# Scores and maxima of an attention stage put into one area of five PSUM banks, with waits kept by bank

## The chip, the cores and the metric

One core of a Trainium2 chip. The metric is the device time of one execution in microseconds (us). PE is the matmul engine (TensorE), PEld its weight load, DVE the vector engine, ACT the scalar engine, POOL GpSimd, SP the queue that issues all transfers. PSUM has eight banks of 512 fp32 columns; matmuls write there, and ACT and DVE read there.

## The reference

Block-sparse attention followed by a two-layer network. 32 heads (batch 4 by 8 heads), 768 positions, head size 64:

```python
scores = scale * np.matmul(q, k.transpose(0, 1, 3, 2))
scores = np.where(mask, scores, -1000000000.0)
scores = scores - np.max(scores, axis=-1, keepdims=True)
attn = np.exp(scores)
attn = attn / (np.sum(attn, axis=-1, keepdims=True) + 1e-09)
x = np.matmul(attn, v)            # then heads side by side: 3072 tokens x 512
h = x @ w_in                      # 512 x 2048
out = (h - np.tanh(h)) @ w_out    # 2048 x 512
```

## The kernel before, in words

The attention runs in 96 steps (`NSTEP`), three to a head; step s works for head s // 3. A step takes two tiles of 128 keys, x = 0 and 1. For each, `scores` writes 128 keys by 768 queries into PSUM as four matmuls (two of 512 columns and two of 256, each pair summing a main and a correction product, L445 and L446), `expo` (ACT, L449) takes the exponential of them into the SBUF tile `pe`, `p_high` (ACT, L455) rounds that to fp16, and `p_low` (POOL, L464) makes the rest. `accum(s)` then multiplies both with the values: 72 short matmuls into the bank `pav` (L478, L481, L482).

The row maxima that are subtracted are found ahead of that. For head h the steps 3h-6 to 3h-4 compute the same scores the other way round, query tile by query tile: `smax(h, t)` is two matmuls (L412) for each of the six tiles t, `maxima` a DVE reduction (L418), two tiles at a time. `turn_max` (PE, L426) transposes the six columns of maxima, `neg_max` (DVE, L430) negates them, and `put_max` (SP, L436) sends them as one row into the operand that `scores` of head h reads. `v_all` and `v_scale` (L382, L386) find a scale for the values of a pair of heads in a corner of the same PSUM place.

PSUM before: `bank0` and `bank1` for the network and the weights, `pst` (two banks) for the scores, of which 768 columns are used, `psm` (three banks, 1536 columns) for the maxima of two tiles, `pav` one. There is one place for scores: `scores` of the next tile waits until `expo` has read the last one.

Every operation is given to a planner (`Plan`) with a due time, an engine, an assumed duration, and names of what it reads and writes (`("pst",)`, `("psm",)`). The planner plays the engines forward, and on each picks the operation with the smallest due time among those that can start within a short time of the earliest. The result is one fixed order for each engine (`in_order`); the waits themselves come from the tile framework, which knows who touched each tile. Where the planner sees PE idle before 110 us of its own time, `KeepBusy` adds dummy matmuls into `pav` (L197).

From step 28 on, parts of the network (`FFN`) are mixed into the attention; until step 25 weights are split into two parts (`convert`, `res_hi`, `res_lo`). What is left of the network runs after the attention, on PSUM that the attention gave back.

Of the kernel before, what the change touches and what calls it, by code (L numbers as in the profile page):

```python
# [22 lines left out]
P = 128  # L23
# [26 lines left out]
BUSY = (14, 110.0, 0.85, 0.2)  # L50
WSTEP = (2, 5, 8, 11, 14, 17, 20, 23)
# [129 lines left out]

class KeepBusy:
# [71 lines left out]
def attention(ctx, tc, plan, qk, v, samp, blocks, xscr, ident, ffn):  # L254
# [4 lines left out]
    pst = ps.tile([P, 1024], F32, name="pst")  # L259
    psm = ps.tile([P, W2], F32, name="psm")  # L260
# [109 lines left out]
    TM, TV = slice(0, 128), slice(128, 256)  # L370
# [7 lines left out]
    def v_tmp(pr):  # L378
        return psm[:, TV] if pr else ffn.hb[1][:, TV]

    def v_all(pr):
        nc.tensor.matmul(v_tmp(pr), lhsT=ams[pr].to_broadcast([P, P]), rhs=ident, start=True, stop=True)  # L382

    def v_scale(pr):
        sb = sbs[pr] = p2.tile([P, 1], F32, tag="sb", name=f"sb{pr}", bufs=4)
        nc.vector.tensor_reduce(out=sb, in_=v_tmp(pr), op=ALU.max, axis=AX.X)  # L386
        sbi = sb.bitcast(I32)
# [17 lines left out]
    def smax(h, t, o=None):  # L405
        s = h % 4
        if t == 0 and h:
            mcs[h] = p2.tile([P, T], F32, tag="mc", name=f"mc{h}", bufs=3)
        b0 = t % 2 * S if o is None else 0
        o = psm if o is None else o  # L410
        for c0, c1 in ((0, 512), (512, S)) if b0 == 0 else ((0, 256), (256, S)):
            nc.tensor.matmul(  # L412
                o[:, b0 + c0 : b0 + c1], lhsT=sB[s][0:88, t * P : (t + 1) * P], rhs=sA[s][0:88, c0:c1], start=True, stop=True
            )

    def maxima(h, t, o=None):
        if o is None:
            nc.vector.tensor_reduce(  # L418
                out=mcs[h][:, t - 1 : t + 1], in_=psm.rearrange("p (x s) -> p x s", x=2), op=ALU.max, axis=AX.X
            )  # L420
        else:
            m = mcs[h][:, t : t + 1] if h else zmc[:, t, 96:97]
            nc.vector.tensor_reduce(out=m, in_=o[:, 0:S], op=ALU.max, axis=AX.X)

    def turn_max(h):
        nc.tensor.transpose(psm[0:T, TM], mcs[h], ident)  # L426

    def neg_max(h):
        nm = p2.tile([T, P], F32R, tag="nm", name=f"nm{h}")
        nc.vector.tensor_scalar(  # L430
            out=nm, in0=psm[0:T, TM], scalar1=-1.0, scalar2=8.0 * PBITS * math.log(2.0), op0=ALU.mult, op1=ALU.add
        )
        nms[h] = nm
# [6 lines left out]
    def scores(s, x):  # L440
# [3 lines left out]
        for q in (slice(0, 512), slice(512, S)):  # L444
            nc.tensor.matmul(pst[:, q], lhsT=sC[c][:, kc], rhs=sD[c][:, q], start=True, stop=False)  # L445
            nc.tensor.matmul(pst[:, q], lhsT=sA[a][0:97, kc], rhs=sB[a][0:97, q], start=False, stop=True)  # L446

    def expo(s, x):
        nc.scalar.activation(out=pe[s % 2][:, x * S : (x + 1) * S], in_=pst[:, 0:S], func=AF.Exp, scale=0.125)  # L449
# [53 lines left out]
    def at(due, f, *args):  # L503
# [32 lines left out]
        elif n == "v_all":  # L536
            eng, dur, r, w = "PE", 0.3, [("am", args[0] % 2)], [("psm",) if args[0] else ("bank", 1)]
        elif n == "v_scale":
            eng, dur, r, w = "DVE", 0.55, [("psm",) if args[0] else ("bank", 1)], [("sb", args[0] % 4)]
# [5 lines left out]
        elif n == "smax":  # L545
            h, t = args[:2]
            eng, dur = "PE", 0.345
            r, w = [(z, h % 4) for z in ("A", "B", "mA", "mB")], [(args[2],) if len(args) > 2 else ("psm",)]
        elif n == "maxima":
            h, t = args[:2]  # L550
            eng, dur = "DVE", dve(768 if len(args) > 2 else 1536) + 0.07
            r, w = [(args[2],) if len(args) > 2 else ("psm",)], [("mc", h % 3, t)]
        elif n == "turn_max":
            eng, dur, r, w = "PE", 0.1, [("mc", args[0] % 3, t) for t in range(T)], [("psm",)]
        elif n == "neg_max":
            eng, dur, r, w = "DVE", 0.25, [("psm",)], [("nm", args[0] % 2)]
        elif n == "put_max":
            dur, r, w = 0.1, [("nm", args[0] % 2)], [("row", args[0] % 4)]
        elif n == "scores":
            s, x = args  # L560
            h = s // 3
            eng, dur, w = "PE", 0.69, [("pst",)]
            r = [(z, h % 4) for z in ("A", "B", "mA", "mB", "row")] + [(z, h % 2, q) for z in "CD" for q in (0, 64)]
        elif n == "expo":
            eng, dur, r, w = "ACT", act(768), [("pst",)], [("pe", args[0] % 2, args[1])]
# [52 lines left out]
    tiles = {"psm": psm, "pst": pst}  # L618
    for t in range(T):
        o, k = ("psm", "pst")[t % 2], -70 + t  # L620
        r = [(z, 0) for z in ("A", "mA", "mB")] + [("B", 0, 0) if t < 2 else ("B", 0)]
        add(k, "PE", 0.345, smax, (0, t, tiles[o]), r, [(o,)])
        add(k + 0.0001, "DVE", dve(768) + 0.07, maxima, (0, t, tiles[o]), [(o,), ("z",)], [("mc", 0, t)])
# [4 lines left out]
    for t in range(T):  # L628
        r = [(z, 1) for z in ("A", "B", "mA", "mB")] + ([] if t else [("pst",)])
        add(0.011 + 0.0002 * t, "PE", 0.345, smax, (1, t), r, [("psm",)])  # L630
        if t % 2:
            at(0.0111 + 0.0002 * t, maxima, 1, t)
# [30 lines left out]
    for h in range(2, NHEAD):  # L663
# [17 lines left out]
    for s in range(NSTEP):  # L681
        for x in range(2):
            at(s + (0.01, 0.065)[x], scores, s, x)
# [423 lines left out]
```

## Time and profile before

| | |
|---|---|
| time, median of 3 runs | 942.32 us (940.71 to 942.59) |
| time of the profiled execution | 942.21 us |
| its span, first to last instruction | 940.4 us |
| PE, DVE, ACT, POOL busy, share of the span | 96%, 76%, 70%, 53% |
| steps 15 to 27 of the attention | 86.1 to 141.4 us of the span |

The span is 1.8 us shorter than the time of the same execution. Matmuls are pipelined, so PE's busy time counts overlaps once and is not its work: how much PE could still take is read from the spacing of its instructions. The shares are averages over stages with different limits.

### The profile page before, as it was taken

The page shows a single profiled execution, that of the slowest core. Times are in us where ns is not written, and L with a number is a line of the kernel's source. Part 1 is how long each engine was busy: PE and PEld are TensorE (multiplying, and loading weights), DVE is VectorE, ACT ScalarE, POOL GpSimd, SP SyncE. Part 2 cuts the span into 40 slices and gives each one's busy share as a digit, 9 for nine tenths or more (in the row PEclk, how much of TensorE's full clock was granted, in tenths as well). Part 3 has the DMA queues.
Part 4 walks back from the last instruction along what each step waited for, and adds up shares of the span by engine and source line. Part 5 has one row for each costly group of instructions (what it writes and reads, how often), then busy time and mean ns, then how long its engine had stood idle before and what let it go on. Part 6 is the DMA issues. An engine that isn't in the chain of part 4 may idle for free.

```text
span 940.4 us, 18434 instructions
## 1 busy us (share of the span) xinstructions
PE 905.7 (96%) x7253; PEld 750.2 (80%) x7253; DVE 711.5 (76%) x1000; ACT 656.9 (70%) x964; POOL 494.2 (53%) x324
## 2 busy tenths in 40 slices
PE   8999989998999999999999999999999999999997
PEld 4778778877888778888877877787888888888885
DVE  6999778779787778887369999976676666666765
ACT  5888888878788888888866566665555555555553
POOL 5678888777867868668843444432222222222221
PEclk9999999999999999999999999999999999999999
DMA  8878669657895666665333222221220401300201
GB/s 216 232 205 211 163 153 299 159 129 209 232 291 132 148 195 160 179 142 179 99 125 105 90 89 90 91 90 45 86 94 1 177 3 52 128 1 1 90 0 45
DMA packets 57678, 120.75 MB, mean 128 GB/s; under 512 B 6170, under 2 KB 26836, under 8 KB 56568
## 3 DMA queue, kind: packets, MB, share of 16 engines
q1 hardware_dynamic: 57592, 119.58, 44.7%
q8 instruction: 57, 0.93, 0.4%
q14 instruction: 29, 0.24, 0.1%
HBM read 55.68 MB, written 26.21 MB: 87 GB/s over the span
## 4 chain that ended last, share of the span: by engine, by line
PE 60%; DVE 24%; ACT 6%; DMA 5%; issue 3%; SPq 1%; POOL 1%; DVEq 0%; POOLq 0%; ACTq 0%
PE bank L811 16%; PE pst L445 7%; PE pst L446 6%; PE psm L412 4%; PE pf L848 4%; PE pf L846 4%; PE pf L847 4%; PE pav L478 3%; ACT pe L449 3%; PE pav L481 3%; PE pav L482 3%; DVE t L837 3%; DVE mc L418 3%; DVE bank L833 3%; DVE bank L835 3%
## 5 line engine op out<-in xcount | busy, mean ns | idle before, releaser
L464 POOL TENSOR_TENSOR pl<-pe,ph 128x768 f16<-128x768 f32 x192 | 329.9, 1732 | 111.9 <-ACT ph L455 76.1
L841 POOL TENSOR_TENSOR gl<-t,gh 128x512 fp32r<-128x512 f32 x96 | 125.8, 1310 | 303.3 <-ACT gh L839 239.0
L449 ACT ACTIVATE pe<-pst 128x768 f32<-128x768 f32 x192 | 155.3, 809 | 64.5 <-PE pst L446 61.3
L418 DVE TENSOR_REDUCE mc<-psm 128x2 f32<-128x1536 f32 x93 | 163.0, 1753 | 38.0 <-PE psm L412 37.5
L455 ACT ACTIVATE ph<-pe 128x768 f16<-128x768 f32 x192 | 159.3, 841 | 2.9
L445 PE MATMUL pst<-slab 128*128 128x512 f32 (+1 forms) x384 | 142.8, 372 | 12.3 <-ACT pe L449 10.1
L831 ACT ACTIVATE u<-u,bias 128x512 f32<-128x512 f32 x96 | 69.4, 723 | 113.1 <-DVE bank L833 113.0
L825 DVE TENSOR_TENSOR t<-t,bank 128x512 f32<-128x512 f32 x96 | 65.7, 684 | 91.3 <-ACT t L823 91.2
L446 PE MATMUL pst<-slab 97*128 97x512 f32 (+1 forms) x384 | 123.6, 343 | 0.0
L478 PE MATMUL pav<-vhl,ph 128*128 128x65 f16 x1152 | 117.6, 194 | 0.0
L481 PE MATMUL pav<-vhl,ph 128*128 128x64 f16 x1152 | 116.7, 195 | 0.2 <-DVE vhl L399 0.2
L482 PE MATMUL pav<-vhl,pl 128*128 128x65 f16 x1152 | 116.2, 193 | 0.0
L478 PEld LDWEIGHTS <-ph 128*128 128x128 f16 x1152 | 105.8, 97 | 7.0 <-issue 3.5
L839 ACT ACTIVATE gh<-t 128x512 fp32r<-128x512 f32 x96 | 60.5, 631 | 68.0 <-DVE t L837 67.9
L482 PEld LDWEIGHTS <-pl 128*128 128x128 f16 x1152 | 107.2, 99 | 0.3 <-issue 0.3
L481 PEld LDWEIGHTS <-ph 128*128 128x128 f16 x1152 | 107.2, 97 | 0.1
L445 PEld LDWEIGHTS pst<-slab 128*128 128x128 f32 x384 | 73.0, 190 | 34.1 <-ACT pe L449 21.1
L412 PE MATMUL psm<-slab 88*128 88x512 f32 (+1 forms) x378 | 87.0, 349 | 3.6 <-DVE mc L418 1.7
L846 PE MATMUL pf<-wx,gh 128*128 128x512 f32 x216 | 84.3, 390 | 2.1 <-DVE ob L907 2.0
L848 PE MATMUL pf<-wx,gl 128*128 128x512 f32 x216 | 84.1, 390 | 0.7 <-POOL gl L841 0.7
L847 PE MATMUL pf<-wx,gh 128*128 128x512 f32 x216 | 84.1, 389 | 0.0
L446 PEld LDWEIGHTS pst<-slab 97*128 97x128 f32 x384 | 73.6, 192 | 11.3
(136 smaller groups left out, 1874.1 us busy)
## 6 DMA issues: line engine op xcount, KB each, us to landing
slab<-hm SPq DMA_DIRECT2D x124, 192.0 KB
slab<-lo SPq DMA_DIRECT2D x63, 192.0 KB
raw<-qk SPq DMA_DIRECT2D x15, 768.0 KB
stage<-w_in SPq DMA_DIRECT2D x16, 512.0 KB
stage<-w_out SPq DMA_DIRECT2D x16, 512.0 KB
xsav<-xbuf SPq DMA_DIRECT2D x4, 2048.0 KB
rawv<-v SPq DMA_DIRECT2D x16, 384.0 KB
xscr<-xq SPq DMA_DIRECT2D x16, 384.0 KB
```

Of the source, the lines that this page charges most:

```text
L412: nc.tensor.matmul(o[:, b0 + c0 : b0 + c1], lhsT=sB[s][0:88, t * P : (t + 1) * P], rhs=sA[s][0:88, c0:c1], start=True, stop=True)
L418: nc.vector.tensor_reduce(out=mcs[h][:, t - 1 : t + 1], in_=psm.rearrange("p (x s) -> p x s", x=2), op=ALU.max, axis=AX.X)
L445: nc.tensor.matmul(pst[:, q], lhsT=sC[c][:, kc], rhs=sD[c][:, q], start=True, stop=False)
L446: nc.tensor.matmul(pst[:, q], lhsT=sA[a][0:97, kc], rhs=sB[a][0:97, q], start=False, stop=True)
L449: nc.scalar.activation(out=pe[s % 2][:, x * S : (x + 1) * S], in_=pst[:, 0:S], func=AF.Exp, scale=0.125)
L455: nc.scalar.activation(out=phs[s][0][:, c], in_=pe[s % 2][:, c], func=AF.Copy)
L464: eng.tensor_tensor(out=pl[:, c], in0=pe[s % 2][:, c], in1=ph[:, c], op=ALU.subtract)
L478: nc.tensor.matmul(oav[:, t, :], lhsT=ph[:, c], rhs=vv[:, 0:65], start=(kt == 0 and t == 0), stop=False, skip_group_check=True)
L481: nc.tensor.matmul(oav[:, t, 0:64], lhsT=ph[:, c], rhs=vv[:, 65:129], start=False, stop=False, skip_group_check=True)
L482: nc.tensor.matmul(oav[:, t, :], lhsT=pl[:, c], rhs=vv[:, 0:65], start=False, stop=last, skip_group_check=True)
L811: self.nc.tensor.matmul(h, lhsT=w[:, cc], rhs=z[:, c, :], start=(c == 0 and x == 0), stop=(c == NCT - 1 and x == 2))
L841: nc.gpsimd.tensor_tensor(out=gl, in0=t, in1=gh.bitcast(F32), op=ALU.subtract)
```

## The change: one area of five banks

`pst` and `psm` become one tile `area` of five banks (0 to 4, 512 columns each). A new class `Banks` remembers which banks each of the last 48 instructions on the area touched, and declares to the tile framework that two instructions of different engines with no bank in common do not depend on each other. The planner's names become one per bank, `("bk", b)`.

Outside of steps 15 to 27 the places are as before: scores in banks 0 and 1 (columns 0 to 767), two tiles of maxima in banks 2 to 4 (1024 to 2559). In steps 15 to 27 (`TWO`) there are two places for scores, columns 0 to 767 (banks 0 and 1) for x = 0 and 768 to 1535 (banks 1 and 2) for x = 1, so that bank 1 is shared; each `scores` is planned as two parts, that in the bank of its own and that in bank 1. The maxima of heads 7 to 11 then have one place, columns 1536 to 2303 (banks 3 and 4), and each tile is reduced by itself. `turn_max` and `v_all` use the end of bank 4 throughout. The core of the diff; the rest carries the new names and arguments through, and in steps 15 to 27 the due times of the second half of `scores` and of every other tile of maxima move (shown in part):

```diff
+TWO = (15, 28)
+class Banks:
+    def __init__(self, tc, t):
+        self.tc, self.t, self.seen = tc, t, deque(maxlen=48)
+    def cols(self, c0, c1, rows=slice(0, P)):
+        self.now = set(range(c0 // 512, (c1 - 1) // 512 + 1))
+        return self.t[rows, c0:c1]
+    def done(self):
+        i = self.tc.nc.cur_bb.bb.instructions[-1]
+        for j, banks in self.seen:
+            if j.engine != i.engine and not banks & self.now:
+                self.tc.declare_no_dep(i, j.name, reason="other banks")
+        self.seen.append((i, self.now))
...
-    pst = ps.tile([P, 1024], F32, name="pst")
-    psm = ps.tile([P, W2], F32, name="psm")
+    area = Banks(tc, ps.tile([P, 5 * 512], F32, name="area"))
...
-    TM, TV = slice(0, 128), slice(128, 256)
+    TM, TV = (2304, 2432), (2432, 2560)
...
+    def two(s):
+        return TWO[0] <= s < TWO[1]
+    def at_max(h, t):
+        if h == 0:
+            return 1024 * (1 - t % 2), (0, 1) if t % 2 else (2, 3)
+        if two(3 * h - 6):
+            return 1536, (3, 4)
+        return (1792, (3, 4)) if t % 2 else (1024, (2, 3))
+    def at_score(s, x):
+        return (S, (1, 2)) if two(s) and x else (0, (0, 1))
...
+    def score_parts(s, x):
+        return ((0, 512), (512, S)) if at_score(s, x)[0] == 0 else ((256, S), (0, 256))
-    def scores(s, x):
+    def scores(s, x, parts):
         h, i = divmod(s, 3)
         a, c = h % 4, h % 2
         kc = slice((2 * i + x) * P, (2 * i + x + 1) * P)
-        for q in (slice(0, 512), slice(512, S)):
-            nc.tensor.matmul(pst[:, q], lhsT=sC[c][:, kc], rhs=sD[c][:, q], start=True, stop=False)
-            nc.tensor.matmul(pst[:, q], lhsT=sA[a][0:97, kc], rhs=sB[a][0:97, q], start=False, stop=True)
+        for c0, c1 in parts:
+            o = at_score(s, x)[0]
+            o = area.cols(o + c0, o + c1)
+            nc.tensor.matmul(o, lhsT=sC[c][:, kc], rhs=sD[c][:, c0:c1], start=True, stop=False)
+            area.done()
+            nc.tensor.matmul(o, lhsT=sA[a][0:97, kc], rhs=sB[a][0:97, c0:c1], start=False, stop=True)
+            area.done()
...
             x = xs[t // 2]
+            if two(3 * h - 6):
+                x += 0.03 * (t % 2)
+                at(x + 0.015, smax, h, t)
+                at(x + 0.016, maxima, h, t, 1)
+                continue
             at(x + 0.015, smax, h, t)
             if t % 2:
-                at(x + 0.02, maxima, h, t)
+                at(x + 0.02, maxima, h, t - 1, 2)
...
-            at(s + (0.01, 0.065)[x], scores, s, x)
+            q = score_parts(s, x)
+            if two(s):
+                for n in range(2):
+                    at(s + (0.01, 0.0105, 0.0215, 0.022)[2 * x + n], scores, s, x, q[n : n + 1])
+            else:
+                at(s + (0.01, 0.065)[x], scores, s, x, q)
```

## Rows read from the trace of the kernel before

**Rows 1.** The page's head: the span, and each engine's busy time, its share of the span and its instructions.

```profile
span 940.4 us, 18434 instructions
PE 905.7 (96%) x7253; PEld 750.2 (80%) x7253; DVE 711.5 (76%) x1000; ACT 656.9 (70%) x964; POOL 494.2 (53%) x324
```

**Rows 2.** Busy time by stretch: start and end of the stretch, its length, then busy us (instructions) of PE, PEld, DVE, ACT and POOL, the granted clock of PE as a share of full speed, the DMA engines' mean busy share, GB/s. The first stretch is steps 15 to 27, the second one step of it (18), the third the rest of the attention, the fourth a part of the network behind it.

```profile
86.10:141.40 55.30, 51.54 (x675) 42.63 (x672) 42.26 (x54) 47.93 (x61) 44.85 (x28) 1.00 0.67 165
98.90:102.80 3.90, 3.71 (x51) 3.14 (x50) 2.62 (x2) 3.10 (x5) 3.32 (x3) 1.00 0.98 199
141.40:472.00 330.60, 319.76 (x3672) 274.70 (x3669) 254.91 (x340) 281.35 (x381) 251.87 (x150) 0.99 0.66 181
650.00:850.00 200.00, 200.00 (x884) 165.46 (x883) 133.65 (x197) 109.33 (x185) 47.38 (x38) 1.00 0.18 64
```

**Rows 3.** ACT in order of time: start us, duration us, instruction, and in brackets the idle time before it and what ended it. Of the 26 intervals from one exponential (L449) to the next between 86.09 and 141.37 us, 16 last 1.93 to 1.94 us; the first rows stand in such a run, the last two are the last such interval.

```profile
98.91 0.81 ACT L449 ACTIVATE pe<-pst 128x768 f32<-128x768 f32 x1 [0.39 <-PE pst L446]
99.62 0.84 ACT L455 ACTIVATE ph<-pe 128x768 f16<-128x768 f32 x1
100.85 0.81 ACT L449 ACTIVATE pe<-pst 128x768 f32<-128x768 f32 x1 [0.39 <-PE pst L446]
...
139.43 0.81 ACT L449 ACTIVATE pe<-pst 128x768 f32<-128x768 f32 x1 [0.25 <-PE pst L446]
...
141.37 0.81 ACT L449 ACTIVATE pe<-pst 128x768 f32<-128x768 f32 x1 [0.26 <-PE pst L446]
```

**Rows 4.** The chain that ended last, in order of time, in step 18: start us, us on the chain, what. The rows left out are the accumulation's other matmuls (until 101.87) and the last three score matmuls.

```profile
98.91 0.82 ACT pe L449
99.73 0.04 issue
99.77 0.50 PE pst L445
100.27 0.24 PE pst L446
100.51 0.12 PE pst L445
100.63 0.12 PE pst L446
100.75 0.05 PE pav L478
...
101.87 0.35 PE pst L445
...
102.79 0.82 ACT pe L449
```

**Rows 5.** Who waited for whom in steps 15 to 27 (86.1 to 141.4 us): us in total, times, longest.

```profile
DVE mc L418 <- PE psm L412: 9.2, 9, 1.9
ACT pe L449 <- PE pst L446: 7.0, 20, 0.7
```

**Rows 6.** Two groups of instructions over the whole span, by shape: the reduction of two tiles, and that of one (head 0): count, busy us, mean ns, idle before.

```profile
L418 DVE TENSOR_REDUCE mc<-psm 128x2 f32<-128x1536 f32 x93 | 163.0, 1753 | 38.0 <-PE psm L412 37.5
L423 DVE TENSOR_REDUCE pe<-psm 128x1 f32<-128x768 f32 x3 | 2.9, 958 | 0.9 <-PE psm L412 0.8
```

**Rows 7.** Instructions in order of time around one single tile of maxima of head 0: its two matmuls, and its reduction.

```profile
10.96 0.59 PE L412 MATMUL pst<-slab 88*128 88x512 f32 x2
...
11.60 0.95 DVE L423 TENSOR_REDUCE pe<-pst 128x1 f32<-128x768 f32 x1
```

**Rows 8.** POOL in order of time: four `p_low` back to back.

```profile
125.13 6.49 POOL L464 TENSOR_TENSOR pl<-pe,ph 128x768 f16<-128x768 f32 x4 [0.23 <-ACT ph L455]
```

**Rows 9.** Single instructions in order of time on the way of the maxima: the first `smax` of head 7; its `turn_max` and `neg_max`, and the first `smax` of head 8; `neg_max` of head 11 and the first exponential of head 11.

```profile
87.05 0.94 PE L412 MATMUL psm<-slab 88*128 88x512 f32 x4
...
97.64 0.27 PE L426 MATMUL psm<-ident,mc 128*6 128x128 f32 x1
...
98.10 0.27 DVE L430 TENSOR_SCALAR nm<-psm 6x128 fp32r<-6x128 f32 x1
...
98.65 0.86 PE L412 MATMUL psm<-slab 88*128 88x512 f32 x4
...
148.24 0.28 DVE L430 TENSOR_SCALAR nm<-psm 6x128 fp32r<-6x128 f32 x1 [0.64 <-PE psm L426]
...
164.23 0.81 ACT L449 ACTIVATE pe<-pst 128x768 f32<-128x768 f32 x1
```

**Rows 10.** A transfer into the same operands as the row of maxima goes to, on the chain that ended last: start us, us, what.

```profile
27.63 3.23 DMA slab<-hm
```

**Rows 11.** Busy time in single microseconds of step 39 (columns as in Rows 2; the granted clock is the third number from the end).

```profile
192.00:193.00 1.00, 1.00 (x4) 0.81 (x3) 1.00 (x1) 0.48 (x1) 1.00 (x2) 0.50 0.84 178
193.00:194.00 1.00, 1.00 (x18) 0.91 (x18) 0.35 (x1) 0.59 (x1) 1.00 (x1) 0.50 0.96 207
194.00:195.00 1.00, 1.00 (x22) 1.00 (x20) 0.00 (x0) 1.00 (x3) 1.00 (x2) 0.50 0.92 243
195.00:196.00 1.00, 1.00 (x9) 0.89 (x7) 0.00 (x0) 1.00 (x3) 1.00 (x2) 0.81 1.06 433
```

**Rows 12.** Busy time by stretch right behind step 27 (columns as in Rows 2).

```profile
141.40:150.00 8.60, 8.56 (x110) 7.37 (x106) 6.18 (x10) 8.17 (x12) 4.95 (x4) 1.00 0.96 289
150.00:160.00 10.00, 10.00 (x113) 8.76 (x112) 8.05 (x9) 8.85 (x13) 9.11 (x5) 1.00 1.01 312
```

More of the change, by code (lines that the diff above doesn't have):

```diff
@@ L1 @@
 import math
+from collections import deque
 from contextlib import ExitStack
@@ L408, in smax, with maxima @@
             mcs[h] = p2.tile([P, T], F32, tag="mc", name=f"mc{h}", bufs=3)
[L409 to L423, printed above, removed]
+        c = at_max(h, t)[0]
+        k = 256 if c % 512 else 512
+        for c0, c1 in ((0, k), (k, S)):
+            o = area.cols(c + c0, c + c1)
+            nc.tensor.matmul(o, lhsT=sB[s][0:88, t * P : (t + 1) * P], rhs=sA[s][0:88, c0:c1], start=True, stop=True)
+            area.done()
+    def maxima(h, t, n):
+        m = mcs[h][:, t : t + n] if h else zmc[:, t, 96:97]
+        c = at_max(h, t)[0]
+        o = area.cols(c, c + n * S).rearrange("p (x s) -> p x s", x=n)
+        nc.vector.tensor_reduce(out=m, in_=o, op=ALU.max, axis=AX.X)
+        area.done()
     def turn_max(h):
-        nc.tensor.transpose(psm[0:T, TM], mcs[h], ident)
+        nc.tensor.transpose(area.cols(*TM, slice(0, T)), mcs[h], ident)
+        area.done()
     def neg_max(h):
         nm = p2.tile([T, P], F32R, tag="nm", name=f"nm{h}")
-        nc.vector.tensor_scalar(
-            out=nm, in0=psm[0:T, TM], scalar1=-1.0, scalar2=8.0 * PBITS * math.log(2.0), op0=ALU.mult, op1=ALU.add
-        )
+        o = area.cols(*TM, slice(0, T))
+        nc.vector.tensor_scalar(out=nm, in0=o, scalar1=-1.0, scalar2=8.0 * PBITS * math.log(2.0), op0=ALU.mult, op1=ALU.add)
+        area.done()
         nms[h] = nm
@@ L559, in at @@
         elif n == "scores":
[L560 removed]
+            s, x, parts = args
             h = s // 3
[L562 removed]
+            c = at_score(s, x)[0]
+            eng, dur = "PE", sum((0.24, 0.45)[c1 - c0 > 256] for c0, c1 in parts)
+            w = [("bk", (c + c0) // 512) for c0, c1 in parts]
             r = [(z, h % 4) for z in ("A", "B", "mA", "mB", "row")] + [(z, h % 2, q) for z in "CD" for q in (0, 64)]
         elif n == "expo":
[L565 removed]
+            s, x = args
+            eng, dur, r, w = "ACT", act(768), [("bk", b) for b in at_score(s, x)[1]], [("pe", s % 2, x)]
         elif n == "p_high":
@@ L617, in attention @@
         at(-76.35 + 0.1 * i if i == 1 else -72.95 + 0.1 * i, fill, i, sA, mk)
-    tiles = {"psm": psm, "pst": pst}
     for t in range(T):
-        o, k = ("psm", "pst")[t % 2], -70 + t
+        k = -70 + t
+        q = [("bk", b) for b in at_max(0, t)[1]]
         r = [(z, 0) for z in ("A", "mA", "mB")] + [("B", 0, 0) if t < 2 else ("B", 0)]
-        add(k, "PE", 0.345, smax, (0, t, tiles[o]), r, [(o,)])
-        add(k + 0.0001, "DVE", dve(768) + 0.07, maxima, (0, t, tiles[o]), [(o,), ("z",)], [("mc", 0, t)])
+        add(k, "PE", 0.345, smax, (0, t), r, q)
+        add(k + 0.0001, "DVE", dve(768) + 0.07, maxima, (0, t, 1), q + [("z",)], [("mc", 0, t)])
         add(k + 0.0002, "PE", 0.3, first_row, (t,), [("mc", 0, t), ("pe", 1, 1)], [("bank", t // 4)])
@@ L628, in attention @@
     for t in range(T):
-        r = [(z, 1) for z in ("A", "B", "mA", "mB")] + ([] if t else [("pst",)])
-        add(0.011 + 0.0002 * t, "PE", 0.345, smax, (1, t), r, [("psm",)])
+        r = [(z, 1) for z in ("A", "B", "mA", "mB")] + ([] if t else [("bk", 0)])
+        add(0.011 + 0.0002 * t, "PE", 0.345, smax, (1, t), r, [("bk", b) for b in at_max(1, t)[1]])
         if t % 2:
-            at(0.0111 + 0.0002 * t, maxima, 1, t)
+            at(0.0111 + 0.0002 * t, maxima, 1, t - 1, 2)
     at(0.0125, turn_max, 1)
```

29 lines of the change are left out of this document (18 added, 11 removed).

## The prediction

> **What bounds the kernel now.** I read the page's head first. PE is busy 96% of 940.4 us [rows 1], which tempts one to call the whole kernel bound by it. The view by stretch corrects that. Behind the attention PE is busy 200.0 of 200 us [rows 2]: nothing that the change touches can shorten that part, but whatever ends the attention earlier moves all of it forward. In steps 15 to 27 (55.3 us, 4.25 a step) every engine has room: ACT 47.9, POOL 44.9, DVE 42.3 us busy [rows 2].
>
> What sets the pace there is a ring. Of 26 intervals between exponentials 16 last 1.94 us, and ACT, though it has nothing else to do, waits for the scores ahead of the next [rows 3]. The chain shows the ring: exponential 0.82, issue 0.04, then four score matmuls on the only score place, 0.50 + 0.24 + 0.12 + 0.12 [rows 4]. The 0.50 is a matmul after a wait; the one that flows behind it has the same 512 columns and takes 0.24. In every second turn the accumulation (100.75 to 101.87, 1.12 us) stands ahead of the scores, and the first score matmul behind it costs 0.35 [rows 4]. By the waits ACT stood 7.0 us for scores in these steps, and DVE 9.2 us for the matmuls of the maxima [rows 5].
>
> **The change part by part.** The profiled execution took 942.21 us (span 940.4 and 1.8 around it), 0.1 below the median of the runs, so the sum is made against 942.2.
>
> *Two places for scores.* The part in a bank of its own (512 columns) can be written while ACT still reads the other place; only the part in bank 1 (256 columns) has to wait for the exponential. ACT runs `p_high` between two exponentials, and in that time PE has only 0.12 + 0.12 us of score matmuls to do [rows 4], so the ring no longer sets the pace. What is late next? Per exponential PE has four flowing score matmuls, 0.24 + 0.24 + 0.12 + 0.12 = 0.72; half an accumulation, 0.56; one `smax`, 0.24 + 0.12 = 0.36; half the extra of the matmul behind the accumulation, (0.35 - 0.24) / 2 = 0.06. That is 1.70. I add 0.07 for a wait of the 0.26 kind (0.50 - 0.24) in one exponential of four: 1.77. POOL needs 6.49 / 4 = 1.62 per exponential [rows 8], ACT 0.71 and at most the 0.84 of `p_high` [rows 3], 1.55. So PE is next, at 1.77 in place of 1.94: 16 x 0.17 = **2.7 us less**. Bounds: nothing, if something else keeps the pace; 16 x 0.32 = 5.1 less, if POOL sets it. I take PE's, since it is the largest of the three works.
>
> *The other ten intervals* hold extra ACT work (weights, the next pair of heads). In the 16 ring intervals ACT waits 0.25 to 0.39, by the middle 16 x 0.32 = 5.1 of the 7.0 us; 1.9 are left for the ten [rows 3, 5]. So between 0 and 1.9 less; ACT's own extra work is due there, and I take about a quarter, **0.5 less**.
>
> *One tile of maxima at a time.* Two single reductions take 2 x 0.958 against 1.753: 0.163 more a pair [rows 6], and five heads (7 to 11) have 15 pairs: 2.4 us more of DVE. The cover is DVE's idle time, 55.3 - 42.3 = 13.0 us [rows 2]; without that cover it is the 2.4. Queued behind a reduction on DVE are the division by the sums, which the accumulator `pav` waits for, and the splitting of operands; they now stand behind 0.96 us instead of 1.75. I take **0.3 more**, bounds 0 to 2.4.
> [...]
>
> *The ring of the maxima.* With one place, the matmuls of a tile wait for the reduction of the one before. From the start of the matmuls to the reduction is 0.64, the reduction 0.95 [rows 7], and 0.04 issue [rows 4]: 1.63 a tile, six tiles 9.8, and 1.0 for `turn_max` and `neg_max` (97.64 to 98.65) [rows 9], which share bank 4: 10.8 us a head. Three steps at 2 x 1.77 are 10.6. So this ring is as long as the new pace, and can be late by some tenths a head; but a head's row is ready well ahead of its use: `neg_max` of head 11 at 148.24, its first exponential at 164.23 [rows 9]. Taken at 0 here; the slower rival below is this ring.
>
> *Waits by bank.* A `scores` in two parts may wait twice. At the chain's 0.04 [rows 4] that is at most 26 x 0.04 = 1.0 us; hidden wherever PE still has matmuls under way, so 0. Outside of steps 15 to 27 the scores keep one place, and the first `smax` of a head need not wait for `neg_max` any more; the 0.55 from `neg_max` to `smax` [rows 9] is a wait of the maxima's chain, which has time to spare: 0. The transfer `put_max` keeps its due time. SP issues it and the operands of later heads in one queue; operand transfers that overwrite a finished head's wait for that head's last `scores`, which comes earlier, not later. The dummy matmuls have less idle time to fill; nobody waits for them.
>
> Sum: -2.7 - 0.5 + 0.3 = -2.9, so **939.3 us**. The later steps must pass it on. In them PE is busy 319.8 of 330.6 us [rows 2], their order is planned anew from a shifted start, and no due time is tied to the clock on the wall, so I let the whole shift through.
>
> **The rivals.**
>
> *The maxima become the pace (slower).* From the first `smax` of head 7 to the first exponential of head 11 before: 164.23 - 87.05 = 77.2 us [rows 9]. Behind the last reduction come `neg_max` 0.28, the transfer, for which a like one took 3.23 [rows 10], and the scores 0.98: 4.5. That leaves 72.7 for five heads, 14.5 a head, less 1.0: 2.25 us a tile. That is the point from which it decides. 1.63 needs PE at once; if a whole accumulation is ahead, it is 1.63 + 1.12 = 2.75, and head 11 comes 5 x (16.5 + 1.0) + 4.5 - 77.2 = 14.8 us late. At 2.4 a tile it is 5 x 15.4 + 4.5 - 77.2 = 4.3 late: **946.5 us**. For it: DVE already waits 9.2 us for these matmuls [rows 5]. Against: the planner knows the wait and places by due time. 0.12.
>
> *Given back (no change).* Right behind step 27 the DMA engines are busy 0.96 and 1.01 of the time [rows 12]. If transfers set the pace there, an earlier start only waits earlier: **942 us**. Against: ACT and PE are nearly as full there (8.85 and 10.00 of 10), and in steps 15 to 27 the DMA share is only 0.67 [rows 2]. 0.20. Here belongs, too, that the declarations don't reach the waits; then PE in steps 15 to 27 would still stand for the exponential ahead of all four score matmuls.
>
> *POOL's pace.* If PE flows without a stall and its parts overlap better than I count, POOL's 1.62 holds: -5.1 - 1.9 = -7.0, **935.2 us**. 0.14.
>
> *The clock.* [...] A new order can add dips or remove one; two more would make it 942.2 - 2.9 + 3.4 = **942.7 us**. Against: PE gets denser in the steps concerned, and the dip in step 39 lies in a part whose places don't change. 0.08.
> [...]
>
> **How the numbers follow.** Forecast 0.46, POOL's pace 0.14, given back 0.20, clock 0.08, maxima 0.12. A measurement of this kernel tells a change from none at about 0.2%, 1.9 us: faster is below 940.4, slower above 944.2. The forecast's own range is 937 to 941; 0.06 of its 0.46 lies above 940.4. So faster 0.40 + 0.14 = 0.54; within 0.06 + 0.20 + half the clock's 0.08 = 0.30; slower 0.12 + 0.04 = 0.16. The lower end lies 0.7 below POOL's pace, 934.5: with one dip gone it would be 935.2 - 1.7 = 933.5, and both together are rare. Above, the forecast with DVE's 2.4 and the waits' 1.0 uncovered is 939.3 + 2.1 + 1.0 = 942.4, and the clock's case 942.7; I end at 943.5, and leave the maxima's rival and part of the clock's outside.
>
> **What would show it.** Right: in steps 15 to 27 the run of 1.94 us intervals between exponentials is gone, most free ones lie near 1.8, ACT's wait for scores is well under 7.0 us, and the steps take about 52.4 us instead of 55.3; single reductions take 0.96 and DVE is busy about 44.7 us. The start of the last stage and the end then move by the same 2.9. Wrong: PE waits for the row of a head (`put_max`) ahead of its first `scores`, or for a reduction ahead of `smax`; intervals of 1.94 remain; steps 28 to 95 take longer than 330.6 us; a granted clock below 1.00 where it was 1.00. The prediction fails above all if steps 15 to 27 gain and the later ones, planned anew, do not pass it on.

## The result: slower, and the profile after

The changed kernel takes 947.34 us (median of 12 runs, 942.79 to 953.13), the kernel before 942.7 in the same session (12 runs, 940.26 to 943.8). The ratio is 1.0051, 95% interval 1.0037 to 1.0065: slower by 4.6 us, where 939.3 was forecast. Executions of one kernel spread over some us, in part by the clock: over the twelve runs of the changed kernel the mean granted clock goes from 0.991 to 0.998, and in the profiled one PE's granted clock is 0.50 in three stretches of 3.4 us, by which an estimated 1.7 us are lost in each (half of 3.4).

The profiled execution took 949.52 us. Its page's head, which answers to [rows 1], and three stretches of it, columns as in [rows 2]: steps 15 to 26, steps 27 to 32, and five microseconds in the latter.

```profile
span 947.7 us, 18458 instructions
PE 912.7 (96%) x7264; PEld 750.0 (79%) x7264; DVE 719.5 (76%) x1015; ACT 657.9 (69%) x964; POOL 499.8 (53%) x324
...
85.10:135.30 50.20, 47.89 (x648) 37.21 (x646) 41.12 (x62) 44.45 (x59) 43.78 (x25) 1.00 0.68 167
135.30:170.90 35.60, 30.22 (x294) 25.33 (x293) 24.23 (x34) 25.27 (x36) 20.61 (x13) 0.90 0.84 245
150.00:155.00 5.00, 1.31 (x38) 1.16 (x36) 1.70 (x2) 2.40 (x4) 4.76 (x3) 1.00 0.96 197
```

The kernel before in the same two groups of steps:

```profile
86.10:137.50 51.40, 48.64 (x654) 40.44 (x650) 40.32 (x50) 44.60 (x57) 41.52 (x26) 1.00 0.66 160
137.50:164.20 26.70, 25.55 (x287) 21.77 (x286) 20.34 (x27) 24.03 (x33) 21.57 (x13) 1.00 0.97 289
```

Steps 15 to 26 gained 1.2 us (51.4 to 50.2). Steps 27 to 32 lost 8.9 (26.7 to 35.6), and PE, there the busiest engine before, was busy for 1.3 of 5 us from 150 on. Followed through the profiled executions by the first exponential of a step, the changed kernel is 1.0 ahead at step 15 (a half-clock stretch at 14 us in the profiled execution of before, 1.7 us lost, explains more than that), 2.2 ahead at step 27, 6.7 late at step 33, 4.7 late at step 36, 5.5 late at the end of the attention, and 7.3 late at the end, where a half-clock stretch at 643 us (1.7 us lost) makes nearly all of the last 1.8. So the question is what happened in steps 27 to 32. Here is DVE of the changed kernel in order of time (columns as in [rows 3]):

```profile
148.56 0.96 DVE L457 TENSOR_REDUCE mc<-area 128x1 f32<-128x768 f32 x1 [1.10 <-PE area L450]
...
153.30 0.95 DVE L393 TENSOR_REDUCE am<-rawv 128x1 f32<-128x768 f32 x1 [3.78 <-DMA rawv<-v]
154.17 0.95 DVE L457 TENSOR_REDUCE mc<-area 128x1 f32<-128x768 f32 x1
...
156.23 0.27 DVE L467 TENSOR_SCALAR nm<-area 6x128 fp32r<-6x128 f32 x1
```

L393 is `v_max(6)`, the maximum over the values of a later pair of heads. It stands in DVE's order between the last two reductions of head 11 (L457) and waits 3.78 us for its load. The last reduction, whose matmuls began at 149.58 and were done when the load landed, stands behind it; `turn_max` of head 11 waits for that reduction, and behind `turn_max` stands everything that PE has to do. The chain that ended last, in the same stretch (columns as in [rows 4]), tells it from the other side:

```profile
144.98 1.03 DVE vhl L422
146.02 7.25 DMA rawv<-v
153.30 0.95 DVE am L393
154.25 0.88 DVE mc L457
155.13 0.04 issue
155.17 0.35 PE area L461
```

The load could start only when DVE had finished with the buffer (`vhl`, L422), and landed 7.25 us later. The waits of 135 to 171 us agree (who, for whom: us in total, times, longest): one stop of about 4 us at L461, which is `turn_max`, seen by PE and by its weight load, beside DVE's 3.8.

```profile
PEld area L461 <- DVE mc L457: 4.8, 3, 4.0
...
PE area L461 <- DVE mc L457: 4.1, 2, 3.9
...
DVE am L393 <- DMA rawv<-v: 3.8, 1, 3.8
```

Right behind the stop, from 155.2 us on, PE's granted clock is 0.50 for 3.4 us; the mean of these five is 0.66:

```profile
155.00:160.00 5.00, 4.83 (x17) 4.07 (x18) 3.37 (x6) 1.66 (x2) 0.69 (x1) 0.66 0.73 260
```

In the kernel before the same `v_max` ran at 152.52, at work at once, and nobody stood behind it who was wanted: a reduction of two tiles ahead of it had ended, and `neg_max` of head 11 had run at 148.24 [rows 9].

```profile
150.86 1.75 DVE L418 TENSOR_REDUCE mc<-psm 128x2 f32<-128x1536 f32 x1
...
152.52 0.94 DVE L374 TENSOR_REDUCE am<-rawv 128x1 f32<-128x768 f32 x1
```

Why did the planner place it so? It takes this load as landed 3.5 us after its issue (141.2 to 144.7 of its own time). With reductions of two tiles it has head 11's last one at 138.4, before it even issues the load. With single ones it has the last one ready at 145.3 only, and sees DVE idle ahead of it: an operation that can start at once (`v_max`, 144.7 to 145.6) goes ahead of one that is due sooner (29.05 against 33.04) but is ready later. The load then came late.

### The profile page after: what moved, and what is told of

Same layout as the page of the kernel before. It is cut to its first block, busy times and chain, and to the rows that moved or that the text cites. A ratio compares the mean times of both kernels' runs of the same rounds, so it can differ in the third digit from the quotient of the medians.

```text
span 947.7 us, 18458 instructions
## 1 busy us (share of the span) xinstructions
PE 912.7 (96%) x7264; PEld 750.0 (79%) x7264; DVE 719.5 (76%) x1015; ACT 657.9 (69%) x964; POOL 499.8 (53%) x324
## 4 chain that ended last, share of the span: by engine, by line
PE 55%; DVE 28%; ACT 5%; DMA 5%; issue 4%; POOL 1%; SPq 1%; DVEq 0%; POOLq 0%; ACTq 0%
PE bank L870 16%; PE area L486 6%; PE area L488 5%; DVE mc L457 5%; PE area L450 4%; PE pf L907 4%; PE pf L905 4%; PE pf L906 4%; DVE t L896 3%; DVE bank L894 3%; DVE bank L892 3%; PE pav L523 3%; DVE t L884 2%; DVE bank L886 2%; PE pav L526 2%
## 5 line engine op out<-in xcount | busy, mean ns | idle before, releaser
L509 POOL TENSOR_TENSOR pl<-pe,ph 128x768 f16<-128x768 f32 x192 | 335.5, 1760 | 110.8 <-ACT ph L500 80.4
L493 ACT ACTIVATE pe<-area 128x768 f32<-128x768 f32 x192 | 155.2, 808 | 63.0 <-PE area L488 57.6
L457 DVE TENSOR_REDUCE mc<-area 128x2 f32<-128x1536 f32 (+1 forms) x108 | 165.4, 1531 | 36.3 <-PE area L450 35.1
L486 PE MATMUL area<-slab 128*128 128x512 f32 (+1 forms) x384 | 141.5, 370 | 6.0 <-ACT pe L493 4.3
L488 PE MATMUL area<-slab 97*128 97x512 f32 (+1 forms) x384 | 124.2, 342 | 0.0
L450 PE MATMUL area<-slab 88*128 88x256 f32 (+1 forms) x384 | 97.1, 357 | 5.7 <-DVE mc L457 3.6
L486 PEld LDWEIGHTS area<-slab 128*128 128x128 f32 x384 | 73.0, 190 | 28.4 <-ACT pe L493 16.3
L488 PEld LDWEIGHTS area<-slab 97*128 97x128 f32 x384 | 73.6, 192 | 9.7
```

The lines of the kernel that those rows point to most:

```text
L450: nc.tensor.matmul(o, lhsT=sB[s][0:88, t * P : (t + 1) * P], rhs=sA[s][0:88, c0:c1], start=True, stop=True)
L457: nc.vector.tensor_reduce(out=m, in_=o, op=ALU.max, axis=AX.X)
L486: nc.tensor.matmul(o, lhsT=sC[c][:, kc], rhs=sD[c][:, c0:c1], start=True, stop=False)
L488: nc.tensor.matmul(o, lhsT=sA[a][0:97, kc], rhs=sB[a][0:97, c0:c1], start=False, stop=True)
L493: nc.scalar.activation(out=o, in_=area.cols(c, c + S), func=AF.Exp, scale=0.125)
L509: eng.tensor_tensor(out=pl[:, c], in0=pe[s % 2][:, c], in1=ph[:, c], op=ALU.subtract)
```

## The experiments

The expectations name the explanations by letters. A: the loss is the place of this one instruction. B: it lies in the change itself, in the single place of the maxima, whose ring (reduce a tile before the next one is written) PE has to follow; beside it stands the cost of the one area and its waits. C: the new order is a little worse everywhere, as any order planned anew may be. D: the ring takes back most of what the second place for scores gives. Ratios are against the kernel before on the same chip (943.91, 943.11 and 942.68 us in the three groups of runs), with 95% intervals.

**The place of `v_max(6)` (e1_seam).** The changed kernel, with this one operation moved in the finished order to right behind `neg_max` of head 11 (the function `move` left out):

```diff
         ops, starts = plan.order()
+        move(ops, starts, ("v_max", (6,)), ("neg_max", (11,)))
```

> The changed kernel with one DVE instruction moved: v_max of pair 6 (the reduction that waits for the values' load) stands behind neg_max of head 11 and no longer ahead of head 11's last reduction of maxima; every other order and all computation stay. Theory A (the time went to that one place in DVE's order: turn_max of head 11, at the head of PE's queue, waits for a reduction that stands behind a load): PE's stop of about 4 us at 150 to 155 us goes, and with it the stretch of half clock that follows it (1.7 us), so 941.5 to 943.5 us against 947.3 for the changed kernel. Theory B (one place for maxima makes their ring the pace in steps 15 to 27): nothing of that is touched, 946 to 948. Theory C (the new order is worse everywhere by a little): 945 to 947.

Measured: 942.44 us, ratio 0.9987 (0.9969 to 1.0005), where the changed kernel had 1.0051 (each against the kernel before on its own chip): 0.64% or 6.0 us for one instruction. DVE in order of time: `neg_max` runs at 150.98 instead of 156.23, and `v_max` behind it without a wait.

```profile
148.91 0.96 DVE L466 TENSOR_REDUCE mc<-area 128x1 f32<-128x768 f32 x1 [0.71 <-PE area L459]
...
150.98 0.27 DVE L476 TENSOR_SCALAR nm<-area 6x128 fp32r<-6x128 f32 x1
151.18 0.93 DVE L402 TENSOR_REDUCE am<-rawv 128x1 f32<-128x768 f32 x1
```

Its stretches, for steps 15 to 26 and 27 to 32:

```profile
85.30:135.50 50.20, 47.89 (x647) 37.19 (x646) 41.06 (x62) 44.40 (x59) 43.87 (x25) 1.00 0.65 166
135.50:164.70 29.20, 27.45 (x294) 22.89 (x293) 24.42 (x34) 25.39 (x36) 21.52 (x13) 1.00 0.97 296
```

The first is that of the changed kernel, 50.20. The second is 29.2 instead of 35.6, at full clock. It is still 2.5 longer than the 26.7 of before. Part of that is work put off. The matmuls of `smax` alone (the same two groups of steps; only PE's and PEld's columns), in the kernel before and in e1_seam:

```profile
86.10:137.50 51.40, 12.25 (x52) 7.95 (x52) 1.00 0.66 160
137.50:164.20 26.70, 4.81 (x21) 3.40 (x22) 1.00 0.97 289
...
85.30:135.50 50.20, 13.69 (x46) 7.21 (x46) 1.00 0.65 166
135.50:164.70 29.20, 7.82 (x28) 4.39 (x28) 1.00 0.97 296
```

Six matmuls, three tiles, have gone from the first group into the second; at the prediction's 0.36 us a tile that is an estimated 1.1 us. So the 1.2 us that steps 15 to 26 gained are hardly a gain: steps 15 to 32 together take 79.4 us in e1_seam and 78.1 in the kernel before, both at full clock. From there on the two orders differ everywhere, and the lead of e1_seam wanders: 0.5 late at step 33, 1.4 ahead at step 36, 5.8 ahead at step 69, 2.4 ahead at the end of the attention, where before's profiled execution has lost 3.4 to two half-clock stretches (at 14 and 192 us) and e1_seam's nothing. The runs leave a gain of 0.13%, and their interval takes in none.

**The same fault put into the kernel before (f1_fault_in_before).** The reverse test: nothing of the change, but `v_max(6)` moved to right ahead of `neg_max(11)`.

```diff
         ops, starts = plan.order()
+        move(ops, starts, ("v_max", (6,)), ("neg_max", (11,)))
```

> The kernel before with one DVE instruction moved the other way: v_max of pair 6 stands ahead of neg_max of head 11 in place of behind head 12's first reduction; all else, layout and order, as before. Theory A: DVE stands some 4 us for the load from about 148 us on, neg_max of head 11 comes that much later, and PE, whose next matmul is the smax of head 12 that waits for it, stops: 4 to 6 us slower than the kernel before, with or without a stretch of half clock. Rival (the stop matters only together with the single place for maxima, or the time was the new order as a whole): at most 1.5 us slower.

Measured: 948.65 us, ratio 1.0068 (1.004 to 1.0095). DVE in order of time, and one of the waits of 141 to 165 us:

```profile
150.24 0.95 DVE L383 TENSOR_REDUCE am<-rawv 128x1 f32<-128x768 f32 x1 [3.46 <-DMA rawv<-v]
151.11 0.27 DVE L439 TENSOR_SCALAR nm<-psm 6x128 fp32r<-6x128 f32 x1
...
PE psm L421 <- DVE nm L439: 3.6, 1, 3.6
```

The wait of 3.46 comes back as PE's 3.6, a half-clock stretch follows at 153 (the mean granted clock of this execution is 0.995), and the kernel falls from 0.8 ahead at step 27 to 4.2 late at step 33, 5.0 us: the wait and one stretch of 1.7 make 5.2. By the mean granted clock of all its six runs f1 loses an estimated 5.5 us to the lower clock, and the kernel before in the same group 2.7: some 2.8 of the 6.2 us between the means are the clock, and the rest is the wait. So the fault alone, in either kernel, is worth about 6 us (6.0 and 6.4 by the ratios). Both directions agree, and this part is shown.

**Stops that nobody stands behind (g1_two_moves, g4_before_moves).** DVE waits for such loads elsewhere too. In e1_seam, `v_max(14)` waits as long as the costly one did, and PE meanwhile is busy throughout (its 384 to 388 us, columns as in [rows 2]):

```profile
387.83 0.95 DVE L402 TENSOR_REDUCE am<-rawv 128x1 f32<-128x768 f32 x1 [3.82 <-DMA rawv<-v]
...
384.00:388.00 4.00, 4.00 (x51) 3.53 (x50) 0.18 (x2) 2.92 (x4) 3.53 (x3) 1.00 0.95 258
```

g1_two_moves is e1_seam with this one moved too; g4_before_moves is the kernel before with two such (2.9 and 1.7 us). The first line is g1's, on top of e1_seam's own move, the other two are g4's:

```diff
+        move(ops, starts, ("v_max", (14,)), ("maxima", (28, 2, 2)))
...
+        move(ops, starts, ("v_max", (12,)), ("maxima", (24, 1)))
+        move(ops, starts, ("v_max", (14,)), ("maxima", (28, 1)))
```

> e1_seam with a second such move: v_max of pair 14, for which DVE stood 3.8 us at 384 to 388 us, behind the next reduction of maxima of head 28. Theory A with the addition that a stop of DVE costs only what PE has to wait for: in e1_seam PE stood only 0.5 to 1 us at that place, so 0 to 1 us less than e1_seam, 941 to 942.5. If every wait of DVE for a load counts: 3 us less, 939 to 940.

> The kernel before with the two reductions that waited longest for the load of the values (pair 12: 2.9 us, pair 14: 1.7 us) moved behind the next reduction of maxima of heads 24 and 28. Theory A with its addition: by the waits PE stood 1.2 us for maxima at the first place, so 0.5 to 1.5 us less than the kernel before. If it is only DVE that waits there: no change.

Measured: 943.0 us, 0.9998 (0.9974 to 1.0021), and 942.37 us, 1.0002 (0.9988 to 1.0016): no gain shows in either, also not the 0.5 to 1.5 us that A gave g4. The intervals exclude that DVE's whole waits count; a gain of 1 us they would not show. A wait of 3.8 us costs 6 us in one place and nothing that can be measured in another; what counts is whether PE stands behind it.

**The ring of the maxima (e3_half_reduce, f6_seam_half).** In both kernels the reductions of heads 7 to 11 read only 384 of the 768 columns, so half of each tile takes no part in the maxima. f6_seam_half has the move of e1_seam as well.

```diff
         o = area.cols(c, c + n * S).rearrange("p (x s) -> p x s", x=n)
+        if two(3 * h - 6) and h:
+            o = o[:, :, 0:384]
```

> The changed kernel in its order, but the reductions of the maxima of heads 7 to 11 read 384 of 768 columns (the maximum is then taken over half the keys; that part is left out): each takes about 0.4 us less, so the ring of a single tile shortens from 1.63 to 1.2 us. Theory B: PE's waits for these reductions in steps 15 to 27 (5.8 us) go, these steps take 2 to 3 us less, and the end follows: 944 to 945.5 us. Theory A: steps 15 to 27 may gain, but the stop behind the load at 150 us starts earlier and ends with the load; at most 1 us comes through, 946 to 948.

> e1_seam and e3_half_reduce together: v_max of pair 6 behind neg_max of head 11, and the reductions of heads 7 to 11 over 384 of 768 columns (the rest of the maximum is left out). Theory D (in steps 15 to 27 the single place for maxima took back most of what the second place for scores gave: 2.6 us by e3_half_reduce's steps): with the stop gone the 2 to 2.6 us now come through, 939 to 940.5 us against e1_seam's 942.4. Rival (the ring is late only within its slack): the same as e1_seam, 941.5 to 943.

Two waits of the changed kernel in steps 15 to 26, and below, steps 15 to 26 of e3_half_reduce with the same wait:

```profile
PEld area L450 <- DVE mc L457: 4.2, 7, 1.0
...
PE area L450 <- DVE mc L457: 1.6, 4, 0.6
```

```profile
86.70:134.30 47.60, 46.58 (x648) 37.28 (x647) 33.67 (x62) 44.05 (x58) 42.53 (x25) 1.00 0.69 174
...
PEld area L450 <- DVE mc L459: 1.9, 4, 0.7
```

PE's weight load waits 4.2 us for reductions ahead of the next `smax` in the changed kernel (the kernel before has 0.3), and 1.9 with half of each reduction. PE's own 1.6 lie within the same stops, so the 5.8 us of the expectation, the sum of both rows, counts them twice. The twelve steps then take 47.6 us instead of 50.2. So the ring of the maxima takes about 2.6 us of what the second score place gives: 51.4 - 47.6 = 3.8 without most of it, 1.2 with it, the three tiles put off included in both. Shorter reductions also leave DVE more time for its other work (busy 33.7 us instead of 41.1); the run does not tell the two apart.

The times: e3_half_reduce 945.6 us, 1.0019 (0.9993 to 1.0044), between the ranges of A and B; f6_seam_half 941.15 us, 0.9989 (0.9964 to 1.0013), above D's range and by the ratio no better than e1_seam. For e3 the reason is in its DVE waits of 136 to 172 us: PE came sooner, the load did not, and `v_max` waited 5.4 instead of 3.8.

```profile
DVE am L393 <- DMA rawv<-v: 5.4, 1, 5.4
```

f6 reaches step 27 at 132.91, 2.6 us before e1_seam, in the same order of instructions. It is 1.5 ahead at step 33, since its `v_max` at 150 waits 2.8 us for the load and PE stands for the reduction behind it, still 1.5 at step 42, and about 0.5 from step 60 on.

```profile
152.73 0.98 PE L459 MATMUL area<-slab 88*128 88x512 f32 x4 [2.71 <-DVE mc L468]
```

So most of what is gained in steps 15 to 26 is given back. For the part at 150 the waits show it; that loads take the rest too is only argued.

**The new area with the old places (e2_one_place).**

```diff
-TWO = (15, 28)
+TWO = (0, 0)
```

> The changed kernel with steps 15 to 27 as all others: one place for scores, two tiles of maxima, but the one area and the waits by bank stay, and the order is planned anew. Theory A: in this order v_max of pair 6 stands behind head 12's first reduction, as in the kernel before, so no stop; 941 to 944 us, equal to the kernel before. Theory B: the same, since the maxima have two tiles again. If waits or bookkeeping of the common area cost something by themselves: 945 or more.

Measured: 946.88 us, 1.0033 (1.0013 to 1.0053), where A and B had 941 to 944: a miss. The expectation kept 945 or more for a cost of the area by itself. The trace shows other stops instead: a `low` of DVE waits 3.8 us for an operand's transfer, and a half-clock stretch follows at 164 (granted clock 0.52 from 164 to 166 us, 0.62 from 166 to 168).

```profile
159.55 3.19 DVE L315 TENSOR_TENSOR lo<-raw,hm 128x1536 fp32r<-128x1536 f32 x1 [3.76 <-DMA slab<-hm]
```

Its steps 15 to 26 took 53.7 us, longer than before's 51.4; PE stood there 2.5 us for reductions ahead of `turn_max` and 1.2 for transfers of operands, where the kernel before has 0.7 and none that shows. As a measure of one part of the change it says little; it says that an order planned anew has such faults in other places too. The area by itself costs no more than the rest of the change gives: e1_seam and n_after have it, and neither shows slower than the kernel before.

**What the waits by bank are worth (f5_no_bank_waits).** e1_seam, in which nothing is declared independent:

```diff
         for j, banks in self.seen:
-            if j.engine != i.engine and not banks & self.now:
-                self.tc.declare_no_dep(i, j.name, reason="other banks")
+            pass
```

> e1_seam without the declarations: the area stays one tile of five banks, in the same order, and the tile framework keeps whatever waits it finds by itself. If it finds them by tile, exponentials, reductions and matmuls wait for one another over the whole area: PE waits for the exponential ahead of smax, DVE's reductions wait for ACT's exponentials; each step gets at least one more such wait of 0.8 us on the path, 96 steps, so 20 to 80 us slower. If it finds them by bank already, the declarations take nothing away and the time is that of e1_seam, 942 to 943.

Measured: 1231.39 us, 1.3068 (1.3013 to 1.3123), 289 us more than e1_seam and far over the 20 to 80 that were expected. Of the waits of the whole run, three by which the two uses of the area hold each other up:

```profile
PEld area L494 <- DVE mc L465: 103.6, 66, 3.1
...
ACT pe L501 <- PE area L458: 86.8, 61, 4.1
...
PEld area L458 <- ACT pe L501: 63.4, 48, 2.5
```

Scores wait for the reductions of the maxima, and the maxima for the exponentials, though they share no column: one tile, one chain. So the declarations do reach the waits in the changed kernel. The mean granted clock of the profiled execution is 0.90, where e1_seam has 0.996, so a part of the 289 us is the clock.

**Other orders (n_after, g2_other_plan, g3_before_other_plan, f7_told).** The planner's allowance for a hop from PE to another engine goes from 0.2 to 0.21 us, in the changed kernel (n_after) and in the kernel before (g3); g2_other_plan is n_after with the moves of e1_seam and g1_two_moves. In f7_told the planner of the changed kernel is told that these loads land 3.5 us later (the last two lines below are f7_told's alone).

```diff
-    HOP = {"PE": 0.2, "ACT": 0.08, "DVE": 0.06, "POOL": 0.08}
+    HOP = {"PE": 0.21, "ACT": 0.08, "DVE": 0.06, "POOL": 0.08}
...
-                end = queue + 0.75
+                end = queue + 0.75 + 3.5 * (o[4].__name__ == "load_v")
```

> The changed kernel planned with another number: the planner's delay from PE to other engines 0.21 instead of 0.20 us; nothing else. v_max of pair 6 still stands ahead of head 11's last reduction. Theory A: the stop stays, 945.5 to 949 us. If an order's luck is worth as much as the difference to be explained, this one can lie anywhere from 941 to 950, and the stop alone would not explain it.

> The changed kernel with the planner told that a load of values (load_v) lands 3.5 us later than it assumed; the order is planned anew, and v_max of pair 6 then stands behind head 12's first reductions. Theory A: no stop at 150 us; what the new order does elsewhere is open, so 940 to 945 us, below the changed kernel's 947.3. If any new order is as likely to be slow as the changed kernel's: anywhere up to 950.

> n_after (the changed kernel planned with 0.21 for PE's delay, 942.6 us) with both moves, v_max of pair 6 behind neg_max of head 11 and of pair 14 behind the next reduction of maxima. n_after has the same order of DVE at 150 us as the changed kernel, but its trace shows a wait for the load of only 0.4 us there; so theory A gives nothing for the first move and 0 to 1 for the second: 941.5 to 942.6. If the position costs by itself, whether the load is late or not: 2 or more less, below 940.6.

> The kernel before planned with 0.21 instead of 0.20 us for PE's delay: how much a new order is worth where nothing else changes. If orders differ by luck alone: 2 us or more to either side of the kernel before. If the kernel before's order is no luck: within 1.5 us of it.

| kernel | us | ratio (95%) |
|---|---|---|
| n_after | 942.64 | 0.9986 (0.9970 to 1.0001) |
| f7_told | 946.59 | 1.0061 (1.0036 to 1.0086) |
| g2_other_plan | 940.66 | 0.9980 (0.9963 to 0.9997) |
| g3_before_other_plan | 943.15 | 1.0009 (0.9993 to 1.0025) |

n_after is as good as e1_seam, with `v_max(6)` in the same bad place. A expected 945.5 to 949 of it: a miss of A as it was first put. In its profiled execution the load came in time but for 0.42 us, and PE is busy in 152 to 155 us, where the changed kernel's stands (n_after first, then the changed kernel, each in its own view by stretch):

```profile
152.00:155.00 3.00, 2.49 (x45) 2.08 (x44) 2.59 (x4) 2.65 (x5) 2.65 (x2) 1.00 0.92 210
```

```profile
152.00:155.00 3.00, 0.00 (x0) 0.00 (x0) 1.70 (x2) 0.40 (x1) 2.98 (x2) 1.00 1.02 216
```

The load had no more time than in the changed kernel: 3.50 us from its issue to the end of the reduction ahead of `v_max` in both (148.49 to 151.99, 146.02 to 149.52). It took less, 3.9 us instead of 7.25. That execution had half clock from 138 to 145 (0.75 from 137 to 140, 0.50 to 143, 0.61 to 146), in which transfers ahead of the load may have drained; this, and whether the load comes in time in the other executions too, is not shown, but the median has no room for a loss of 6 us. So the place is not wrong in itself; it is wrong when the load comes late. f7_told is a miss too (940 to 945 expected): no `v_max` waits for its load any more, but the order found under the new assumption is 2.6 us late at step 15 and 6.8 at step 33. Better knowledge of one duration did not make a better order.

g2_other_plan is the fastest of all, faster than the kernel before by 0.2%, if barely. In the same group of runs the kernel before with the same planner setting had 943.15, so with that setting the change is worth 2.5 us. n_after, without the moves, has nearly the same ratio. Moves and setting were picked, so that the change is worth this in a well-laid order is a fair reading and not a proof.

## Why the prediction was wrong, point by point

**The step that failed** is the last one of the sum: "their order is planned anew from a shifted start, and no due time is tied to the clock on the wall, so I let the whole shift through". Due times don't tie a step to the wall clock, but loads do: a load starts when its buffer is free (at 146.02 us, where `vhl` ends, in the changed kernel) and takes its own time, 3.4 to 8.7 us in the runs here. `v_max`, which waits for one, was not among the work that I named as sharing DVE with the reductions. That it could come to stand ahead of a reduction that PE waits for was not priced: 6 us (e1_seam, f1_fault_in_before). The text did say that the prediction fails above all if steps 15 to 27 gain and the later ones don't pass it on, and that is what happened; but the rival that stood for it, "given back", had no change as its time, and no term for a stop of PE.

**Two places for scores: the ring went, the gain did not come.** Of 26 intervals between exponentials 3 are near 1.94, where there were 16 [rows 3]. The free ones did not settle at 1.77: they lie between 1.47 and 3.29, many of them at 2.0 to 2.3. Of the 2.9 us expected for 13 steps, steps 15 to 26 gave 1.2, and three tiles of `smax`, an estimated 1.1 us, are put off in that. **The mis-sized term is the ring of the maxima, "taken at 0"**: it cost about 2.6 (e3_half_reduce). My working had the warning in it: a ring of 10.8 us a head against a pace of 10.6. I let it off because a head's row is ready long ahead of its use. But it was not the head's row that was late. PE's order is fixed, so PE itself stood at the next `smax` for the reduction, with the scores behind it. With most of the ring gone, the gain less the tiles put off is an estimated 2.7 us (3.8 - 1.1), near the forecast's 2.9. Slack at the end of a chain does not protect the engine in the middle of it.

**The rival "the maxima become the pace"** was therefore half right: PE waits for reductions ahead of `smax`, as I wrote that it would show, but at some 2.6 us in the twelve steps and not through a late row of head 11. That its 946.5 lies near the 947.34 measured is chance: the stop behind a load made the time, which that rival did not have.

**Single reductions.** Over the whole span (columns as in [rows 6]):

```profile
L457 DVE TENSOR_REDUCE mc<-area 128x1 f32<-128x768 f32 x30 | 28.6, 954 | 9.4 <-PE area L450 8.9
```

954 ns each, so a pair costs 2 x 0.954 - 1.753 = 0.155 us more, against 0.163 in the sum; 15 pairs are 2.3 us. The duration was right. What the single reductions cost was more than DVE's time: the planner put `v_max` into a hole between the short instructions.

**Waits by bank** reach the chip as declared (without the declarations e1_seam takes 289 us more, f5_no_bank_waits); that part of the rival "given back" is out.

**The clock.** The granted clock is 1.00 in steps 15 to 26 in both kernels, also where the scores of the changed one go round three banks. The stretches at half clock came elsewhere, two of them behind waits of PE (at 138 and 155, 0.81 and 3.86 us). The 1.7 us a dip in the clock rival's 3.4 and in the lower end of the forecast's range is what the clock takes over [rows 11]; the changed kernel's stretches at 138, 155 and 643 us are of that size, 3.4 us at 0.50 each. The rival put two more of them into the run; the profiled executions have one more, three against before's two (at 14 and 192 us), and the stop of PE, which that rival did not have. For the sum of the profiled executions: steps 27 to 32 lost 8.9, of which two half-clock stretches (138 and 155) are 3.4, what e1_seam still loses there 2.5 (the tiles put off among it), and the stop itself the remaining 3.0.

**Given back** fits what is left when the fault is gone: e1_seam and g1_two_moves come to within 0.2% of the kernel before, and f6_seam_half's lead on e1_seam shrinks from 2.6 us to 0.5 by step 60. For e1_seam itself there was little to give back.

## What to carry to other kernels

When a change makes an engine's instructions shorter or frees a place, look at what the order will put into the new holes: an instruction that waits for a transfer cost nothing that shows here where nobody wanted what stood behind it (3.82 us of wait in e1_seam; 943.0 us with it moved, 942.44 without). Where the bounding engine needed the next instruction in that queue, it cost nearly its whole wait (3.78 us of DVE and 3.86 of PE in the changed kernel, 3.46 and 3.6 in f1_fault_in_before), and in both a stretch of half clock as well, 1.7 us. List those instructions (here sixteen `v_max`) before costing the shift that later steps "pass on". Count a ring at the engine that closes it, not at the slack of its last product. And when a group of steps gets shorter, count its instructions: work may only have been put off.

## What the runs showed of the hardware that was not expected

The same load took 7.25 us in the changed kernel, while in the kernel before `v_max` had its data no later than 4.86 us after the issue (147.66 to 152.52). The DMA engines were 0.95 busy over the first, and 0.91 over the second, so the mean share alone doesn't tell a slow load from a fast one. The bytes moved do. From the issue of this load to its landing (`v_max` starts at once behind it) in the changed kernel, n_after, f1_fault_in_before and f6_seam_half, the last two numbers being the DMA engines' share and GB/s:

```profile
146.02:153.27 7.25, 5.29 (x83) 4.57 (x79) 2.40 (x3) 5.65 (x9) 4.82 (x3) 1.00 0.95 235
...
148.49:152.41 3.92, 3.81 (x40) 3.19 (x36) 2.39 (x3) 3.26 (x7) 1.93 (x2) 1.00 0.90 268
...
146.84:150.24 3.40, 0.98 (x8) 0.69 (x6) 0.00 (x1) 2.39 (x4) 2.65 (x2) 1.00 0.81 275
...
141.39:150.06 8.67, 8.63 (x102) 7.54 (x98) 3.54 (x8) 7.22 (x11) 6.24 (x4) 1.00 1.01 287
```

Length times rate is 1.7, 1.1, 0.9 and 2.5 MB for a load of 0.39 MB (384 KB). So the slow ones did not move at a much lower rate; they shared the time with more of other transfers. And an issue 4.6 us earlier (f6 against the changed kernel) brought the data 3.2 us earlier only, with the load 1.4 us slower. What sets that amount in each order is not worked out here.

The clock fell behind one wait and not behind its like. At 138 us PE of the changed kernel and PE of e1_seam do the same work in the same order, and both wait 0.81 us for a reduction (the ring of the maxima). Rows in order of time, the changed kernel first:

```profile
137.78 0.70 PE L450 MATMUL area<-slab 88*128 88x512 f32 x2 [0.81 <-DVE mc L457]
138.28 0.63 PE L486 MATMUL area<-slab 128*128 128x512 f32 x1
```

```profile
137.99 0.62 PE L459 MATMUL area<-slab 88*128 88x512 f32 x2 [0.81 <-DVE mc L466]
138.44 0.40 PE L495 MATMUL area<-slab 128*128 128x512 f32 x1
```

In the first the granted clock is 0.50 from 138.2 us on and the same score matmul takes 0.63 us; in the second the clock is 1.00 (137 to 140 us) and it takes 0.40. Nor did f6_seam_half's clock fall behind PE's 2.71 us at 150 (1.00 from 150 to 160). The stretch at 138 lasts 3.4 us and costs an estimated 1.7, so single executions of one kernel can't tell a gain of 0.2% from none.
